# Routing steps of a token group dealt out evenly over the six half-units that may carry them

## The chip, the cores and the metric

The kernel runs on one core of a Trainium2 chip. The metric is the device time of one launch in microseconds (us), the median of the runs shown. Before the change it is 934.42 us (three runs: 934.04, 934.42, 937.76). The profile that is read below is one further execution with its own time, 937.85 us.

The engines are TensorE (PE, with its weight loads as PEld), VectorE (DVE), ScalarE (ACT), GpSimd (POOL) and SyncE (SP), which issues most DMAs. Each engine works through its own list of instructions in order.

## The reference

Linear attention feeds a mixture of experts that sends each token to one expert:

```
proj = x @ w_phi                       # x is q or k: batch 8, heads 8, seq 576, head_dim 64; 128 features
proj -= max|proj| over the features
phi  = [exp(proj), exp(-proj)]         # 256 features
kv = phi(k)^T @ v ; z = sum phi(k)     # per batch and head
out = (phi(q) @ kv) / (phi(q) @ z + 1e-6)

x = out as 4608 tokens x 512
logits = x @ w_gate                    # 8 experts
e = argmax(logits) ; g = softmax(logits)[e]
y = g * (relu(x @ w1[e]) @ w2[e])      # 512 -> 1024 -> 512
```

## The kernel before

**Units and groups.** The attention is cut into 16 units. A unit is two batch rows (a group) and two heads (a pair); four units in a row make a group, and there are four groups. A unit has nine chunks of 128 tokens, taken in pieces 8, 0, 2, 4, 6 (`PIECES`: the last chunk alone, then four pairs of chunks). In what follows "k2" is the piece that begins with chunk 2 of k, "q2" that of q. Every fp32 matmul operand is split in a high part and a remainder (`xh`, `xl`; `kh`, `kl`; `vh`, `vl`; in the experts `wh`, `wl`), and ACT makes the high part, DVE or POOL the remainder.

**One piece.** PE projects (L246 to L248, `ps_proj`, two PSUM buffers), DVE takes the largest magnitude (`mx`, L252) and subtracts it (`t`, L253). For k, ACT makes the exponentials `e` and then `kh` (L273), and POOL or DVE makes `kl` (L275). For q, PE transposes `t` into `pt` (L284) and ACT makes the exponentials `qp` from it. So PE works on a piece, hands it to DVE, and needs DVE's `t` back twice: for the transposes `pt` of a q piece, and before the PSUM buffer of the piece may be used again two pieces later.

**Beside the features** of one unit, PE carries the products of the unit before: `pk` (phi(k)^T v, L315), `pf` (with w_gate folded in, L341) and `pn` (phi(q) times that, L363). Each unit is emitted in two halves, `first_half` and `second_half`, lists of such matmuls that `merge` zips with the feature pieces by their costs. DVE normalises `pn` into `xrow` and the logits' parts `lgc`.

**Routing.** When the first unit of a group has been emitted, the routing of the group before is put on a list of 27 steps, `deferred` (function `route`): logits, the largest, shift, candidates, first of the largest, one-hot, a sum, three empty steps, `count_ranks` (ten small matmuls into `prk` and DVE's `rks`), an empty step, `rank` (`rki`), `rank_parts` (`rkb`, L652, and `rki` again, L653), `rank_values` (POOL casts `blk` and `rkr`, L656 and L657), nine `select` steps (each one DVE instruction `sel_p` and one POOL instruction `sel_h`, L671), and three steps for the gate. For the last full group eleven steps of `lead` follow: they look for the most used expert (`pc`, `lead_e`), mark its first tokens (`bl`, L746), find their rows (54 small matmuls into `pl`) and gather them (`xg`, L774). Three such lists are worked off, in units 5 and 6, in units 9 and 10, and in units 13 to 15. The function `spread` inserts steps between the items of a half: one behind every sixth item, from the seventh on.

**What sets the order.** The lists only say in which order instructions are emitted. A scheduler then places them on each engine by dependences, priorities and its own idea of costs, and it moves an instruction forward when its engine would otherwise be free. What stands where is therefore read from the built program; the section on the change shows such places.

Of the kernel before, what the change touches and what calls it, by code (L numbers as in the profile page):

```python
# [27 lines left out]
NPR = H // 2  # L28
# [19 lines left out]
def tile_linear_attention_moe(  # L48
# [142 lines left out]
    NLAST0, NLAST, AHEAD = 4, 4, 5  # L191
# [69 lines left out]
    def k_features(st, c0, n):  # L261
        t = project(st, "k", c0, n)
        m = 2 * n
        e = work.tile([P, 4, 2, F], F32, name="e", bufs=2)
        A.activation(e[:, 0:m, 0, :], t[:, 0:m, :], AF.Exp)
        A.activation(e[:, 0:m, 1, :], t[:, 0:m, :], AF.Exp, scale=-1.0)
        st["e", c0] = e
# [38 lines left out]
    def kv_steps(st, bb):  # L306


        def step(hh, i, c, j):
            vh, vl = st["v"]  # L310
            if (hh, i, j) == (0, 0, 0):
                st["pk", bb] = ps_kv.tile([P, 2, 2 * F], F32, name="pk", tag="pk")
            n = D if j == 1 else D + 1
            kh, kl, s0 = st["kp", c]
            return T.matmul(  # L315
                st["pk", bb][0:n, hh, :],
                (vl if j == 1 else vh)[:, 2 * (c + (bb if c == 8 else 0)) + hh, 0:n],
                (kl if j == 2 else kh)[:, s0 + hh].rearrange("p s f -> p (s f)"),
                start=(hh, i, j) == (0, 0, 0),
                stop=(hh, i, j) == (1, 4, 2),  # L320
            )

        return [
            (120, lambda a=(hh, i, c, j): step(*a))
            for i, c in enumerate(CHUNKS[bb])
            for hh in range(2)
            for j in range(3)
        ]

    def kv_copy(st, bb):  # L330
        kvT = sm.tile([D + 1, 2, 2 * F], F32, name="kvT")
        A.copy(kvT, st["pk", bb][0 : D + 1])
        st["kvT", bb] = kvT

    def fold_steps(st, bb):


        def step(hh, s):
            if (hh, s) == (0, 0):
                st["pf"] = ps_kv.tile([P, 2, 2, W], F32, name="pf", tag="pk")  # L340
            m = T.matmul(  # L341
                st["pf"][:, hh, s, :],
                st["kvT", bb][:, hh, s * F : (s + 1) * F],
                fold[:, 2 * st["pr"] + hh, :],
                start=True,
                stop=True,
            )
            if (hh, s) == (1, 1):
                st["kf", bb] = sm.tile([P, 2, 2, W], F32, name="kf", bufs=3)
                with tc.high_priority(offset=200):  # L350
                    V.tensor_copy(st["kf", bb], st["pf"])
            return m

        return [(168, lambda a=(hh, s): step(*a)) for hh in range(2) for s in range(2)]

    def num_steps(st, chunks):


        def step(c, hh, bb, s):
            if c % 3 == 0 and hh == 0 and s == 0:  # L360
                st["pn"] = ps_nm.tile([P, 6, W], F32, name="pn")
            qp, s0 = st["qp", c]
            m = T.matmul(  # L363
                st["pn"][:, 2 * (c % 3) + hh, :],
                qp[:, s, s0 + hh, :] if c < 8 else qp[:, s, hh, bb : bb + 2].rearrange("p b q -> p (b q)"),
                st["kf", bb][:, hh, s, :],
                start=(s == 0 and (c < 8 or bb == 0)),
                stop=(s == 1 and (c < 8 or bb == 1)),
            )
            if c % 3 == 2 and hh == 1 and s == 1 and (c < 8 or bb == 1):  # L370
                normalize(st, c - 2, st["pr"])
                if c == 8:
                    eng = G if st["g"] == NG - 1 and st["pr"] == 2 else nc.sync
                    store_rows(st["g"], st["x"], st["pr"] * P, P, eng=eng)
            return m

        return [
            (186, lambda a=(c, hh, bb, s): step(*a))
            for c in chunks
            for hh in range(2)  # L380
            for bb in ([c // 4] if c < 8 else [0, 1])
            for s in range(2)
        ]
# [35 lines left out]
    def ordered(items):  # L419


        def go(f):
            m = f()
            if behind_order[0] is not None:
                tc.add_manual_dep(
                    m.ins,
                    behind_order[0].ins.name,
                    mybir.DependencyInfo(mybir.DependencyClass.NoSync, mybir.DependencyReason.DATA),
                    reason="order of the products",
                )  # L430
            behind_order[0] = m

        return [(t, lambda f=f: go(f)) for t, f in items]

    def half(kv, fo, nu, copy):

        res = kv[:CUT1] + zipped(kv[CUT1:CUT2], fo) + kv[CUT2:CUT3] + zipped(kv[CUT3:], nu)
        return ordered(res) + [(0, copy)]

    def first_half(prev):  # L440
        return half(
            kv_steps(prev, 1), fold_steps(prev, 0), num_steps(prev, range(4)), lambda: kv_copy(prev, 1)
        )

    def second_half(cur, prev):
        if prev is None:
            return ordered(kv_steps(cur, 0)) + [(0, lambda: kv_copy(cur, 0))]
        return half(
            kv_steps(cur, 0), fold_steps(prev, 1), num_steps(prev, range(4, 9)), lambda: kv_copy(cur, 0)
        )  # L450

    def run(steps):
        for f in steps:
            f()

    def spread(items, steps):

        res, k = [], 0
        for i, it in enumerate(items):
            res.append(it)  # L460
            if i >= 6 and i % 6 == 0 and k < len(steps):
                res.append((0, steps[k]))
                k += 1
        del steps[:k]
        return res
# [19 lines left out]
    def feature_items(st, u):  # L485
        ks = {c: (330 * n, lambda c=c, n=n: k_features(st, c, n)) for c, n in PIECES}
        kps = {c: (0, lambda c=c, n=n: k_parts(st, c, n)) for c, n in PIECES}
        qs = {c: (550 * n, lambda c=c, n=n: q_features(st, c, n)) for c, n in PIECES}

        def do(f, *a):  # L490
            return (0, lambda: f(*a))

        if u == 0:
            st["ranges"] = RANGES0
            return first_items(st, ks, kps, qs, do)
        st["ranges"] = [(0, CUT), (CUT, NC * P)]
        items = []
        for part in range(2):
            for x in "kq":
                items += [do(load, st, x, part), do(split, st, x, part, A, G)]  # L500
            if part == 0:
                items += [ks[8], qs[8], kps[8], ks[0], qs[0], kps[0]]
        items.append(do(v_parts, st, u))
        return items + [f for c in (2, 4, 6) for f in (ks[c], qs[c], kps[c])]

    def merge(a, b):
        ta, tb = sum(x[0] for x in a) or 1, sum(x[0] for x in b) or 1
        i = j = 0
        ca = cb = 0.0
        while i < len(a) or j < len(b):  # L510
            if j >= len(b) or (i < len(a) and ca / ta <= cb / tb):
                ca += a[i][0]
                a[i][1]()
                i += 1
            else:
                cb += b[j][0]
                b[j][1]()
                j += 1
# [273 lines left out]
    deferred, prev = [], None  # L792
# [4 lines left out]
    feats = feature_items(units[0], 0)  # L797
    for u, st in enumerate(units):
        steps = deferred if u % NPR else []
        nxt = feature_items(units[u + 1], u + 1) if u + 1 < len(units) else []  # L800
        if u == 0:
            merge(feats[:-NLAST0], [])
            feats = feats[-NLAST0:]
        else:
            merge(feats[:-NLAST], spread(first_half(prev), steps))
            feats = feats[-NLAST:]
        merge(feats + nxt[:AHEAD], spread(second_half(st, prev), steps))
        feats = nxt[AHEAD:]
        prev = st
        if u % NPR == 0 and u > 0:  # L810
            run(deferred)
            deferred = route(st["g"] - 1, units[u - 1]["lgc"], 0, NC)
            if st["g"] == NG - 1:
                deferred += lead()
# [81 lines left out]
    st = {}  # L896
# [322 lines left out]
```

## Time and profile before

| | |
|---|---|
| median of three runs | 934.42 us |
| profiled execution, its own time | 937.85 us |
| its span, first to last instruction | 935.9 us |
| PE busy | 895.8 us (96%) |
| DVE, ACT, POOL busy | 593.1, 591.8, 499.1 us |

The attention units run until about 430 us of the span (the last `pn` matmuls), and the experts after that. A matmul is pipelined, so its end is modelled and neighbours overlap. The DVE and POOL durations are spans: an instruction that its engine has begun but that is kept from going on is shown long. [...]

### The profile page before, as it was taken

The page shows a single profiled execution, that of the slowest core. Times are in us where ns is not written, and L with a number is a line of the kernel's source. Part 1 is how long each engine was busy: PE and PEld are TensorE (multiplying, and loading weights), DVE is VectorE, ACT ScalarE, POOL GpSimd, SP SyncE. Part 2 cuts the span into 40 slices and gives each one's busy share as a digit, 9 for nine tenths or more (in the row PEclk, how much of TensorE's full clock was granted, in tenths as well). Part 3 has the DMA queues.
Part 4 walks back from the last instruction along what each step waited for, and adds up shares of the span by engine and source line. Part 5 has one row for each costly group of instructions (what it writes and reads, how often), then busy time and mean ns, then how long its engine had stood idle before and what let it go on. Part 6 is the DMA issues. An engine that isn't in the chain of part 4 may idle for free. (4 is left out here: it accounts for less than half of the span.)

```text
span 935.9 us, 18394 instructions
## 1 busy us (share of the span) xinstructions
PE 895.8 (96%) x6824; PEld 839.3 (90%) x6824; DVE 593.1 (63%) x1016; ACT 591.8 (63%) x895; POOL 499.1 (53%) x355
## 2 busy tenths in 40 slices
PE   5999998999899999999799999999999999999995
PEld 4899998999899989999699999999999999987884
DVE  6777778777887778859754444444444444457850
ACT  5877775878677766756455555555555555568961
POOL 6666668766686669553433333333333333346641
PEclk9999999999999999999999999999999999999998
DMA  4333333333223333143133143431434634664100
GB/s 125 117 105 100 99 106 94 99 98 94 67 89 104 105 105 92 42 150 116 42 126 117 46 158 114 158 113 46 152 113 158 216 114 149 225 208 133 45 24 15
DMA packets 64349, 102.38 MB, mean 109 GB/s; under 512 B 10687, under 2 KB 28479, under 8 KB 64257
## 3 DMA queue, kind: packets, MB, share of 16 engines
q1 hardware_dynamic: 56928, 80.34, 27.7%
q0 software_dynamic: 6720, 20.80, 7.1%
q8 instruction: 54, 0.88, 0.4%
q14 instruction: 39, 0.31, 0.1%
q10 hardware_dynamic: 608, 0.05, 0.0%
HBM read 136.74 MB, written 20.26 MB: 168 GB/s over the span
## 5 line engine op out<-in xcount | busy, mean ns | idle before, releaser
L928 DVE TENSOR_TENSOR wl<-raw,wh 128x1024 fp32r<-128x1024 f32 x137 | 185.7, 1368 | 139.0 <-ACT wh L927 135.6
L927 ACT CAST wh<-raw 128x1024 fp32r<-128x1024 f32 x184 | 191.5, 1049 | 96.1 <-PE po L992 68.3
L928 POOL TENSOR_TENSOR wl<-raw,wh 128x1024 fp32r<-128x1024 f32 x47 | 116.6, 2486 | 173.5 <-ACT wh L927 166.1
L363 PE MATMUL pn<-kf,qp 128*128 128x73 f32 x1024 | 155.3, 254 | 0.0
L970 PE MATMUL pm<-xh,wh 128*128 128x256 f32 x544 | 153.7, 283 | 0.7 <-ACT xh L952 0.7
L971 PE MATMUL pm<-xl,wh 128*128 128x256 f32 x544 | 154.1, 283 | 0.2 <-DVE xl L953 0.2
L972 PE MATMUL pm<-xh,wl 128*128 128x256 f32 x544 | 153.9, 283 | 0.0
L363 PEld LDWEIGHTS pn<-kf,qp 128*128 128x128 f32 x1024 | 149.3, 191 | 0.2
L252 DVE TENSOR_REDUCE mx<-ps_proj 128x4 f32<-128x512 f32 (+1 forms) x160 | 100.6, 631 | 66.3 <-PE ps_proj L248 65.7
L275 POOL TENSOR_TENSOR kl<-e,kh 128x1024 fp32r<-128x1024 f32 x47 | 112.2, 2388 | 40.6 <-ACT kh L273 38.5
L235 POOL TENSOR_TENSOR xl<-xr,xh 128x512 fp32r<-128x512 f32 (+2 forms) x62 | 88.1, 1420 | 52.7 <-ACT xh L234 52.5
L991 PE MATMUL po<-wl,hh 128*128 128x512 f32 x272 | 107.3, 394 | 3.0 <-DVE wl L928 3.0
L990 PE MATMUL po<-wh,hh 128*128 128x512 f32 x272 | 109.8, 404 | 0.0
L970 PEld LDWEIGHTS pm<-xh,wh 128*128 128x128 f32 x544 | 104.1, 191 | 3.3 <-ACT xh L952 0.9
L971 PEld LDWEIGHTS pm<-xl,wh 128*128 128x128 f32 x544 | 104.1, 191 | 2.8 <-DVE xl L953 0.4
L992 PE MATMUL po<-wh,hl 128*128 128x512 f32 x272 | 106.6, 392 | 0.0
L972 PEld LDWEIGHTS pm<-xh,wl 128*128 128x128 f32 x544 | 104.1, 191 | 0.0
L253 DVE TENSOR_TENSOR t<-ps_proj,mx 128x512 f32<-128x512 f32 (+1 forms) x160 | 101.0, 633 | 3.4
L246 PE MATMUL ps_proj<-w_hi,xh 128*128 128x256 f32 x288 | 92.8, 322 | 7.9 <-DVE xh L234 4.3
L315 PE MATMUL pk<-kh,vl 128*64 128x256 f32 x320 | 98.2, 307 | 2.2 <-POOL vl L303 2.2
L315 PE MATMUL pk<-kh,vh 128*65 128x256 f32 x320 | 98.1, 306 | 1.0 <-DVE vh L302 1.0
L315 PE MATMUL pk<-kl,vh 128*65 128x256 f32 x320 | 97.7, 305 | 1.1 <-POOL kl L275 0.7
(217 smaller groups left out, 2023.0 us busy)
## 6 DMA issues: line engine op xcount, KB each, us to landing
raw<-w SPq DMA_DIRECT2D x184, 512.0 KB
vt<-vv SPq DMA_DIRECT2D x16, 640.0 KB
x_dram<-xrow SPq DMA_DIRECT2D x30, 256.0 KB
xr<-kT SPq DMA_DIRECT2D x15, 320.0 KB
xr<-qT SPq DMA_DIRECT2D x15, 320.0 KB
xr<-kT SPq DMA_DIRECT2D x17, 256.0 KB
xr<-qT SPq DMA_DIRECT2D x17, 256.0 KB
x_dram<-xrow SPq DMA_DIRECT2D x32, 32.0 KB
```

Of the source, the lines that this page charges most:

```text
L253: V.tensor_tensor(t[:, 0 : 2 * n, :], psv, mx[:, 0 : 2 * n].unsqueeze(2).to_broadcast([P, 2 * n, F]), op=ALU.subtract,)
L275: eng.tensor_tensor(kl, e[:, 0:m], kh, op=ALU.subtract)
L315: return T.matmul(st["pk", bb][0:n, hh, :], (vl if j == 1 else vh)[:, 2 * (c + (bb if c == 8 else 0)) + hh, 0:n], (kl if j == 2 else kh)[: ...
L363: m = T.matmul(st["pn"][:, 2 * (c % 3) + hh, :], qp[:, s, s0 + hh, :] if c < 8 else qp[:, s, hh, bb : bb + 2].rearrange("p b q -> p (b q)" ...
L927: A.copy(th, raw[k])
L928: (G if k in (POOL_LO if u else POOL_LO0) else V).tensor_tensor(tl, raw[k], th, op=ALU.subtract)
L970: T.matmul(pm[:, i], th, xh[:, k, :], start=(k == 0), stop=False)
L971: T.matmul(pm[:, i], th, xl[:, k, :], start=False, stop=False)
L972: T.matmul(pm[:, i], tl, xh[:, k, :], start=False, stop=(k == KD - 1))
L990: T.matmul(po, hh[:, i, r], th[:, c], start=(i == j == 0), stop=False)
L991: T.matmul(po, hh[:, i, r], tl[:, c], start=False, stop=False)
L992: T.matmul(po, hl[:, i, r], th[:, c], start=False, stop=(i == 1 and j == 3))
```

## The change

`spread` gets the number of half-units that are left for the list, `halves`, and inserts that share of the steps, rounded up, at even distances in the half, instead of one behind every sixth item. For the first unit after the list is made there are six halves left, then five, and so on down to one.

```diff
-    def spread(items, steps):
-
+    def spread(items, steps, halves):
+
+        n = -(-len(steps) // halves) if halves else 0
         res, k = [], 0
         for i, it in enumerate(items):
             res.append(it)
-            if i >= 6 and i % 6 == 0 and k < len(steps):
+            while k < n and (k + 1) * len(items) <= (i + 1) * (n + 1):
                 res.append((0, steps[k]))
                 k += 1
         del steps[:k]
         return res
...
         steps = deferred if u % NPR else []
+        halves = 2 * (NPR - u % NPR) if u % NPR else 0
...
-            merge(feats[:-NLAST], spread(first_half(prev), steps))
+            merge(feats[:-NLAST], spread(first_half(prev), steps, halves))
             feats = feats[-NLAST:]
-        merge(feats + nxt[:AHEAD], spread(second_half(st, prev), steps))
+        merge(feats + nxt[:AHEAD], spread(second_half(st, prev), steps, max(0, halves - 1)))
```

A first half has 51 items and a second 59. Before, they took eight and nine steps, so the 27 steps were emitted in 8, 9, 8 and 2, and the 38 with `lead` in 8, 9, 8, 9 and 4. Now the 27 go out in 5, 5, 5, 4, 4, 4 and the 38 in 7, 7, 6, 6, 6, 6. The instructions are the same ones. The steps from the logits to the one-hot and the gate keep their places on DVE and POOL: these lists are alike row by row in both programs up to and with `RECIPROCAL se`. What moves stands behind them.

DVE before, where the ranks of the first group are made, in the second half of unit 5 (`t_2086` is k6 and `t_2137` q6 of that unit):

```order
L253 TENSOR_TENSOR t_2086<-ps_proj_2078,mx_2085 128x512
L644 TENSOR_TENSOR rks_2126<-prk_2115,onehot_138 128x72
L648 TENSOR_REDUCE rki_2165<-rks_2126 128x9
L252 TENSOR_REDUCE mx_2136<-ps_proj_2129 128x4
L652 TENSOR_SCALAR rkb_2173<-rki_2165 128x9
L253 TENSOR_TENSOR t_2137<-ps_proj_2129,mx_2136 128x512
L390 TENSOR_SCALAR rec_2157<-pn_2064 128x6
L653 TENSOR_SCALAR rki_2165<-rki_2165 128x9
```

DVE now, where the same steps stand, in the first half of unit 6 (`t_2250` is k0, `t_2285` q0, `t_2334` k2, `t_2356` q2):

```order
L253 TENSOR_TENSOR t_2250<-ps_proj_2242,mx_2249 128x512
L645 TENSOR_TENSOR rks_2270<-prk_2259,onehot_138 128x72
L252 TENSOR_REDUCE mx_2284<-ps_proj_2277 128x4
L649 TENSOR_REDUCE rki_2345<-rks_2270 128x9
L253 TENSOR_TENSOR t_2285<-ps_proj_2277,mx_2284 128x512
L252 TENSOR_REDUCE mx_2333<-ps_proj_2326 128x4
L653 TENSOR_SCALAR rkb_2374<-rki_2345 128x9
L253 TENSOR_TENSOR t_2334<-ps_proj_2326,mx_2333 128x512
L654 TENSOR_SCALAR rki_2345<-rki_2345 128x9
L252 TENSOR_REDUCE mx_2355<-ps_proj_2348 128x4
L672 TENSOR_SCALAR sel_p_142<-iota_pb_130,rkr_2430,part1_133 128x128
L253 TENSOR_TENSOR t_2356<-ps_proj_2348,mx_2355 128x512
```

The rank steps have moved by about half a unit, and the nine `sel_p`, one row of nine before, are now dealt out one by one between the `mx` and `t` of q2, k4, q4, k6 and q6. The second group has the same rows in unit 10.

POOL before, from the remainders at the end of unit 5 on:

```order
L303 TENSOR_TENSOR vl0_158<-vt_2340,vh0_156 128x1280
L617 CAST base_b_3484<-base_144 128x8
L656 CAST blk_141<-rkb_2173 128x9
L235 TENSOR_TENSOR xl_2331<-xr_2328,xh_2330 128x512
L657 CAST rkr_2183<-rki_2165 128x9
L671 TENSOR_SCALAR sel_h_143<-iota_pb_130,rkr_2183,hbase_135 128x128 x4
L275 TENSOR_TENSOR kl_2195<-e_2089,kh_2194 128x1024
L671 TENSOR_SCALAR sel_h_143<-iota_pb_130,rkr_2183,hbase_135 128x128 x5
L235 TENSOR_TENSOR xl_2337<-xr_2334,xh_2336 128x512
L275 TENSOR_TENSOR kl_2325<-e_2278,kh_2324 128x1024
```

POOL now, the same stretch (`kl_2307` is that of k0 of unit 6, made from `t_2250`):

```order
L303 TENSOR_TENSOR vl0_158<-vt_2322,vh0_156 128x1280
L235 TENSOR_TENSOR xl_2313<-xr_2310,xh_2312 128x512
L275 TENSOR_TENSOR kl_2172<-e_2081,kh_2171 128x1024
L618 CAST base_b_3555<-base_144 128x8
L275 TENSOR_TENSOR kl_2307<-e_2253,kh_2306 128x1024
L235 TENSOR_TENSOR xl_2319<-xr_2316,xh_2318 128x512
L657 CAST blk_141<-rkb_2374 128x9
L658 CAST rkr_2430<-rki_2345 128x9
L672 TENSOR_SCALAR sel_h_143<-iota_pb_130,rkr_2430,hbase_135 128x128 x9
L235 TENSOR_TENSOR xl_2554<-xr_2551,xh_2553 128x640
L275 TENSOR_TENSOR kl_2443<-e_2394,kh_2442 128x1024
L235 TENSOR_TENSOR xl_2560<-xr_2557,xh_2559 128x640
```

The cast `rkr`, which the first `sel_p` on DVE waits for, now stands behind `kl` of k0 and one more `xl`. The nine `sel_h` follow each other without a break, and the three remainders behind them come in one go.

In the third list (unit 13) the ranks stay in the second half. There DVE now has `rkb`, `rki` and five `sel_p` in a row ahead of k8 of unit 14, and POOL stands like this:

```order
L235 TENSOR_TENSOR xl_5235<-xr_5232,xh_5234 128x512
L657 CAST blk_141<-rkb_5127 128x9
L275 TENSOR_TENSOR kl_5099<-e_5001,kh_5098 128x1024
L658 CAST rkr_5189<-rki_5091 128x9
L672 TENSOR_SCALAR sel_h_143<-iota_pb_130,rkr_5189,hbase_135 128x128 x9
```

Before, `blk`, an `xl` of 512 and `rkr` followed each other there; now a `kl` of 1024 stands between `blk` and `rkr`. The steps of `lead` have moved from the last pieces of unit 14 and the first of unit 15 to the middle and the end of unit 15: `bl` from ahead of k8 to ahead of k4, and the 54 `pl` matmuls from behind q0's projection to around q6's transposes.

## Rows read from the trace of the kernel before

**Rows 1.** The page, part 1: busy time, share of the span, instructions
```profile
PE 895.8 (96%) x6824; PEld 839.3 (90%) x6824; DVE 593.1 (63%) x1016; ACT 591.8 (63%) x895; POOL 499.1 (53%) x355
```
**Rows 2.** Stretches: length, busy us (instructions) of each engine, PEclk, DMA share, GB/s
```profile
141.50:145.00 3.50, 3.50 (x19) 3.50 (x20) 3.26 (x9) 2.12 (x4) 2.29 (x3) 0.52 0.26 75
...
170.00:180.00 10.00, 10.00 (x96) 9.99 (x96) 8.15 (x18) 9.59 (x16) 7.18 (x4) 1.00 0.20 55
```
**Rows 3.** Who waited for whom: us in total, times, longest us
```profile
PE pt L284 <- DVE t L253: 9.1, 7, 1.5
```
**Rows 4.** PE in order of time: start us, us, instruction [idle before <-releaser]
```profile
154.56 0.66 PE L284 MATMUL pt<-ident,t 128*128 128x128 f32 x4 [1.52 <-DVE t L253]
...
390.70 0.39 PE L246 MATMUL ps_proj<-w_hi,xh 128*128 128x256 f32 x1 [0.46 <-DVE t L253]
```
**Rows 5.** DVE in order of time, the ranks of the first group
```profile
151.59 2.33 DVE L652 TENSOR_SCALAR rkb<-rki 128x9 int32<-128x9 int32 x1
154.50 0.93 DVE L653 TENSOR_SCALAR rki<-rki 128x9 int32<-128x9 int32 x1
...
156.14 2.15 DVE L671 TENSOR_SCALAR sel_p<-iota_pb,rkr,part 128x128 bf16<-128x128 bf16 x9
```
**Rows 6.** POOL in order of time, the same stretch and the unit behind it
```profile
151.19 2.69 POOL L303 TENSOR_TENSOR vl<-vt,vh 128x1280 fp32r<-128x1280 f32 x1
...
154.13 1.27 POOL L235 TENSOR_TENSOR xl<-xr,xh 128x512 fp32r<-128x512 f32 x1
155.49 0.19 POOL L657 CAST rkr<-rki 128x9 f32<-128x9 int32 x1
155.79 3.41 POOL L671 TENSOR_SCALAR sel_h<-iota_pb,rkr,hbase 128x128 bf16<-128x128 bf16 x4
...
165.84 1.29 POOL L235 TENSOR_TENSOR xl<-xr,xh 128x512 fp32r<-128x512 f32 x1
167.09 2.40 POOL L275 TENSOR_TENSOR kl<-e,kh 128x1024 fp32r<-128x1024 f32 x1
169.44 1.58 POOL L235 TENSOR_TENSOR xl<-xr,xh 128x640 fp32r<-128x640 f32 x1
```
**Rows 7.** One tile's instructions: duration ns min/median/max, first and last start us
```profile
L652 DVE TENSOR_SCALAR rkb<-rki x5: 165/1984/2343, 151.6 to 439.8; 128x9 int32<-128x9 int32 x3, 128x6 int32<-128x6 int32 x1, 128x3 int32<-128x3 int32 x1
...
L671 DVE TENSOR_SCALAR sel_p<-iota_pb,rkr,part x31: 299/307/434, 156.1 to 441.3; 128x128 bf16<-128x128 bf16 x31
```
**Rows 8.** DVE in order of time in unit 6: t of k0, q2 and q4
```profile
163.00 0.68 DVE L253 TENSOR_TENSOR t<-ps_proj,mx 128x512 f32<-128x512 f32 x1
...
167.84 0.69 DVE L253 TENSOR_TENSOR t<-ps_proj,mx 128x512 f32<-128x512 f32 x1
...
173.39 0.69 DVE L253 TENSOR_TENSOR t<-ps_proj,mx 128x512 f32<-128x512 f32 x1
```
**Rows 9.** ACT in order of time: the split ahead of kh of k0, unit 6, and kh
```profile
165.03 0.62 ACT L234 CAST xh<-xr 128x512 fp32r<-128x512 f32 x1
165.56 1.04 ACT L273 CAST kh<-e 128x1024 fp32r<-128x1024 f32 x1
```
**Rows 10.** PE in order of time: transposes of q2 and q6, unit 6; k0's projection, unit 14
```profile
168.81 0.60 PE L284 MATMUL pt<-ident,t 128*128 128x128 f32 x4
...
178.90 0.60 PE L284 MATMUL pt<-ident,t 128*128 128x128 f32 x4
...
365.62 0.37 PE L246 MATMUL ps_proj<-w_hi,xh 128*128 128x256 f32 x1
```
**Rows 11.** POOL in order of time, the third list, between blk and rkr
```profile
359.45 1.26 POOL L235 TENSOR_TENSOR xl<-xr,xh 128x512 fp32r<-128x512 f32 x1
```
**Rows 12.** The lead's steps: DVE's bl, and POOL's issue of a gather
```profile
386.86 2.41 DVE L746 TENSOR_SCALAR bl<-choice,ld 128x27 f32<-128x27 f32 x1
...
396.09 1.29 POOL L774 DMA_INDIRECT xg<-x_dram,gidx  x1 [6.85 <-DVE gidx L763]
```
**Rows 13.** PE in order of time: first transposes of a gathered block
```profile
417.93 0.27 PE L950 MATMUL px<-ident,xg 128*128 128x128 f32 x1
```

## The prediction

> **What bounds the kernel now.** I read the busy times first: PE is busy for 895.8 us, 96% of the span, far ahead of DVE with 63% [rows 1]. So an engine other than PE costs time only where PE waits for it. The view of stretches says where that is: in a stretch of a unit without routing PE is busy for 10.00 of 10.00 us with DVE at 8.15 [rows 2]. The list of waits then shows one kind that returns: transposes `pt` that wait for DVE's `t`, 9.1 us in seven waits, the longest 1.5 [rows 3]. In order of time they lie where routing is worked off, two to a group and a short one at the lead.
>
> The last one of each group lies at the ranks, and its cause can be read off DVE's rows beside POOL's. DVE's `rkb`, nine numbers per partition, takes 2.33 us and ends at 153.92, within 0.04 of the end of POOL's `vl` (151.19 and 2.69) [rows 5, 6]. `rki` takes 0.93 and ends with POOL's `xl` (154.13 and 1.27). The same `rkb` takes 165 ns where POOL does no such work [rows 7]. So DVE's small step is held until POOL's subtraction is through, `t` of q6 comes late, and PE waits 1.52 us [rows 4]. It is so in all three groups.
>
> [...]
>
> **The first chain of a group does not move.** Logits to one-hot and the gate keep their rows on DVE and POOL although they are emitted later: the scheduler moves them forward as before. Their waits, one of the seven in each group, and what follows stay. [...]
>
> **What is removed.** The waits at the ranks: 3 x 1.52 = 4.6 us, since `rkb` and `rki` no longer stand ahead of q6's `t`, or, in the third group, not ahead of one that is near. In the lead, `bl` was held for 2.41 us [rows 12] ahead of k8 and made PE wait 0.46 [rows 4]; it now stands where POOL's list is thinner. Together 5.1 us.
>
> **What is added in the first and the second group: a wait for `rkr`.** DVE's first `sel_p` stands ahead of `t` of q2 and waits for `rkr`. On POOL `rkr` stands behind `kl` of k0, `xl` and `blk`, and that `kl` waits for `kh` of the very k0 that DVE has just done. Counted from the end of k0's `t` (163.68 [rows 8]): `kh` ends at 166.60, of which 0.53 goes since ACT now has the split behind it [rows 9], so at +2.4. Then 2.40 for `kl`, 1.29 for `xl`, 0.19 each for `blk` and `rkr` [rows 6] and some 0.3 for handing over: +6.8. `sel_p` 0.30 [rows 7] and `t` 0.69: `t` of q2 ends at +7.8. PE had its transposes of q2 at 168.81, +5.1 [rows 10], and the ten `prk` matmuls now ahead of them give it perhaps 0.3 more. That is a wait of 2.4; k0's `t` may come a little earlier against PE, as the nine `sel_p` (2.15) no longer stand ahead of it. I take 2.0, bounds 1.2 and 2.4. Behind the waiting `sel_p` stand q2's `t` and all later pieces; PE needs them at once.
>
> **Added in the same groups: selects held behind the burst.** Nine `sel_h` in a row last 9 x 0.85 = 7.7 us (3.41 for four [rows 6]), to +14.5. Then POOL has `xl` to +16.1, `kl` to +18.5 and `xl` to +20.1 back to back (1.58, 2.40, 1.58). DVE's `t` of q4 ended at 174.08, +10.4 [rows 8]; with PE's wait of 2.0 and four `sel_p` (0.24 each) now at +13.4. A copy and `mx` of k6 bring +14.5. There follow `sel_p`, `t` of k6, `sel_p`, `mx` of q6, `sel_p`, `t` of q6, each `mx` and `t` about 0.7. If the first slips in ahead of `xl`, the second is held to +16.1 and the third, by `kl`, to +18.5, and q6's `t` ends at about +19.5. PE wants it at 178.90, +15.2, plus 2.0 and 0.3: +17.5. Wait 2.0. If the first is held too, 3.6; if none is, +17.5 and nothing. No row shows a `sel_p` beside an `xl` or `kl`: its longest is 0.43 [rows 7]. The nearest row is `rkb`, the same operation on DVE, held in full, so I take 2.0 and keep 0 and 3.6 as ends. POOL itself can bear the burst: the remainders it delays feed projections of the next unit.
>
> **Added in the third group.** There `rkb` ends with `xl` at about 360.5 (360.71 before [rows 11], less a little for a shorter list). `blk`, `kl`, `rkr` and handing over take 0.19 + 2.40 + 0.19 + 0.3: DVE stands still until about 363.6. Five `sel_p` (1.2), then `mx`, `sel_p` and `t` of k8, half pieces: 366.0. PE began k0's projection, which needs k8's PSUM buffer, at 365.62 [rows 10], and would now at 364.1. Wait 1.9, and about 0.6 more at q8 behind a further `sel_p`. I take 2.5, bounds 1.0 and, if a later `sel_p` is held by a `kl`, 4.8.
>
> **The lead.** Its steps now stand between k4's and q4's `mx` and `t`: 0.3, bounds 0 and 1. The gathers start some 17 us later than at 396.09 [rows 12]. The `pl` matmuls end at about 412, POOL's list is free by 413, and PE wants the first block at 417.93 [rows 13]: hidden by a few us, so nothing.
>
> **The sum.** -5.1 + 2 x (2.0 + 2.0) + 2.5 + 0.3 = +5.7 us. The clock is not in it: a wait of 1.5 alone brought no slow stretch, two near each other did in two groups of three. I take no change, bounds -3.4 (both stretches go) and +5 (one more per group). The profiled execution took 937.85 us, 1.95 outside its span, so by it the sum is 943.5. The median shown is 3.43 lower, 934.42, and runs of one kernel lie between 934.04 and 937.76; on that base the forecast is **940.1 us**.
>
> **Rivals.**
> *The selects slip through.* For: beside `sel_h` they are not held, and they are bf16 while all held steps shown have 32-bit operands. Against: same operation as `rkb`. Then 2 x 2.0 + 2.5 + 0.3 - 5.1 = +1.7: about 936.
> *The new waits find cover and the clock stays up.* The price is decided by k0's `t`: if it comes a microsecond earlier against PE, the wait for `rkr` falls to its bound, 1.2, and with no select held the sum is -5.1 + 2.4 + 1.0 + 0 = -1.7; without the slow stretches -5.1, about 929. For it: DVE has 2.15 us less ahead of k0. Against: `rkr` hangs on k0's own `kh`, so POOL's 4.1 us come in any case. This is the one on the other side; say 930.
> *The gather is late.* If `pl` or POOL's list ends 4 us later than I count, the first block lands behind 417.93, and each us is PE's. Price about 4: 944.
> *Every POOL instruction holds a DVE select, `sel_h` too.* Five `sel_p` stand in the burst, and each would wait up to 0.85 us, about 0.4 on average: 2 us per group, 6 in all, 946. The trace speaks against it, as said. [...]
>
> **How the numbers follow.** Forecast 0.55 (936 to 946 for itself), selects slip through 0.25, cover 0.10, gather late 0.05, every instruction holds 0.05. The range for 8 in 10 is 932 to 946: the low end takes in the second rival and part of the third, the bounds of the single waits (3.4 to 17.8 added, 5.1 removed) would reach from 929 to 952 if all fell one way. A change under 0.5% (4.7 us) can't be told from none. Faster by more than that: most of the cover case and a little of the next, 0.11. Slower by more, above 939.1: two thirds of the forecast and the two small rivals, 0.48. Within: 0.41.
>
> **What would show it.** In the changed profile: `choice`, `oh_b` and the gate at the times of before, with the slow clock behind them; no wait of PE at q6 of units 5 and 9; DVE idle ahead of a first `sel_p` with `rkr` as releaser, some 2 us, and PE waiting at q2 (or at k4's projection) of units 6 and 10; single `sel_p` of 1 to 2.4 us that end with an `xl` or `kl` of POOL; in unit 14 DVE idle for about 3 us ahead of five `sel_p`. I am wrong if all `sel_p` stay at 0.3 us, if `rkr` comes before DVE has done `mx` of q2, or if PE's waits in the attention fall below the 9.1 us of before.

## The result and the profile after

The changed kernel took 948.93 us in the median of four executions (943.99, 945.92, 951.95, 959.24), against 934.29 for the kernel before: slower, 1.0122 times the time, with an interval of 1.0092 to 1.0153. The comparison leaves out executions over 1.5% above the fastest of their kernel as disturbed, here the 959.24 and in the run once more 957.44 and 959.32, though the experiments show below that such times are most likely the kernel's own, so its ratios are on the low side. The profiled execution is the fastest, 943.99 us with a span of 941.9, so 6.0 us of span over before. The forecast was 940.1, and 943.5 for the profiled execution.

PE's busy time is up by 2.5 us on [rows 1], which fits a further stretch at the lower clock (below), and its waits are up. Part 1 of the page, then the two groups of PE's waits for `t` between 120 and 460 us (total, times, longest):

```profile
PE 898.3 (95%) x6824; PEld 840.9 (89%) x6824; DVE 595.5 (63%) x1016; ACT 592.8 (63%) x895; POOL 498.0 (53%) x355
```
```profile
PE pt L284 <- DVE t L253: 11.6, 9, 2.3
PE ps_proj L246 <- DVE t L253: 3.9, 6, 1.4
```

The first line answers to [rows 3] with 9.1; the second kind came to 2.3 in four waits before. Together 15.5 against 11.4. In order of time the waits lie here (start, duration, instruction, idle before and releaser); the first is the old one of the first chain, the next three are unit 6, the last three unit 14:

```profile
140.83 1.08 PE L284 MATMUL pt<-ident,t 128*128 128x128 f32 x4 [1.45 <-DVE t L253]
166.30 0.35 PE L246 MATMUL ps_proj<-w_hi,xh 128*128 128x256 f32 x1 [0.34 <-DVE t L253]
168.40 0.63 PE L284 MATMUL pt<-ident,t 128*128 128x128 f32 x4 [1.15 <-DVE t L253]
181.10 0.66 PE L284 MATMUL pt<-ident,t 128*128 128x128 f32 x4 [2.25 <-DVE t L253]
...
371.84 0.39 PE L246 MATMUL ps_proj<-w_hi,xh 128*128 128x256 f32 x1 [1.42 <-DVE t L253]
373.44 0.44 PE L284 MATMUL pt<-ident,t 128*128 128x128 f32 x2 [0.21 <-DVE t L253]
381.14 0.63 PE L284 MATMUL pt<-ident,t 128*128 128x128 f32 x4 [0.21 <-DVE t L253]
```

Unit 10 repeats unit 6 with 0.36, 1.16 and 2.27. The waits at the ranks (1.52, 1.54 and 1.53) and that of 0.46 [rows 4] are gone, with another of 0.23 at the lead. So 9.4 us came (3.74 and 3.79 in the two groups, 1.84 in the third) and 5.3 went.

Why q2 and q6 are late is read off DVE's and POOL's rows of unit 6, side by side. DVE:

```profile
163.36 2.21 DVE L653 TENSOR_SCALAR rkb<-rki 128x9 int32<-128x9 int32 x1
165.48 0.68 DVE L253 TENSOR_TENSOR t<-ps_proj,mx 128x512 f32<-128x512 f32 x1
166.08 0.72 DVE L654 TENSOR_SCALAR rki<-rki 128x9 int32<-128x9 int32 x1
...
167.31 0.34 DVE L672 TENSOR_SCALAR sel_p<-iota_pb,rkr,part 128x128 bf16<-128x128 bf16 x1
...
175.26 1.36 DVE L672 TENSOR_SCALAR sel_p<-iota_pb,rkr,part 128x128 bf16<-128x128 bf16 x1
176.54 0.68 DVE L253 TENSOR_TENSOR t<-ps_proj,mx 128x512 f32<-128x512 f32 x1
177.14 1.82 DVE L672 TENSOR_SCALAR sel_p<-iota_pb,rkr,part 128x128 bf16<-128x128 bf16 x1
...
179.48 0.97 DVE L672 TENSOR_SCALAR sel_p<-iota_pb,rkr,part 128x128 bf16<-128x128 bf16 x1
```
POOL:
```profile
163.16 2.38 POOL L275 TENSOR_TENSOR kl<-e,kh 128x1024 fp32r<-128x1024 f32 x1 [1.89 <-ACT kh L273]
165.49 1.28 POOL L235 TENSOR_TENSOR xl<-xr,xh 128x512 fp32r<-128x512 f32 x1
...
166.87 0.19 POOL L658 CAST rkr<-rki 128x9 f32<-128x9 int32 x1
167.17 7.87 POOL L672 TENSOR_SCALAR sel_h<-iota_pb,rkr,hbase 128x128 bf16<-128x128 bf16 x9
175.00 1.56 POOL L235 TENSOR_TENSOR xl<-xr,xh 128x640 fp32r<-128x640 f32 x1
176.53 2.38 POOL L275 TENSOR_TENSOR kl<-e,kh 128x1024 fp32r<-128x1024 f32 x1
178.87 1.53 POOL L235 TENSOR_TENSOR xl<-xr,xh 128x640 fp32r<-128x640 f32 x1
180.36 2.68 POOL L303 TENSOR_TENSOR vl<-vt,vh 128x1280 fp32r<-128x1280 f32 x1
```

Add start and duration in each row. `rkb` ends at 165.57, `kl` at 165.54; `rki` at 166.80, the 512 `xl` at 166.77; the three long `sel_p` at 176.62, 178.96 and 180.45, POOL's `xl`, `kl`, `xl` at 176.56, 178.91 and 180.40. Each step of DVE is kept until POOL's subtraction is through. Beside the nine `sel_h` a `sel_p` takes 0.34. Over the whole kernel (duration in ns, least, median, most) the longest `sel_p` went from 434 [rows 7] to 2054 (it stands behind the `t` of q6, where PE no longer waits for it):

```profile
L672 DVE TENSOR_SCALAR sel_p<-iota_pb,rkr,part x31: 266/340/2054, 167.3 to 447.3; 128x128 bf16<-128x128 bf16 x31
```

In unit 14 DVE stands still for `rkr` as forecast:

```profile
369.61 1.29 DVE L672 TENSOR_SCALAR sel_p<-iota_pb,rkr,part 128x128 bf16<-128x128 bf16 x5 [2.56 <-POOL rkr L658]
```

The clock makes up the rest. These are the stretches of the attention with the lower clock (columns as in [rows 2]; PEclk, third from the end, is the granted TensorE clock as a share of the full one, and in 2.50 us inside each of the three it is 0.50):

```profile
140.00:145.00 5.00, 4.17 (x25) 4.20 (x25) 4.56 (x12) 2.60 (x5) 3.23 (x4) 0.66 0.19 52
181.00:186.00 5.00, 4.90 (x33) 4.90 (x34) 2.86 (x6) 1.09 (x2) 5.00 (x3) 0.66 0.63 168
287.00:292.00 5.00, 4.78 (x31) 4.78 (x32) 2.97 (x6) 1.08 (x2) 5.00 (x3) 0.66 0.59 165
```

Each costs 5 x 0.34 = 1.7 us. The new two stand behind the waits at q6; before, there were two, behind the first chains of groups one and three, 3.50 us at 0.52 [rows 2] and 4.00 at 0.57:

```profile
346.00:350.00 4.00, 3.03 (x15) 3.06 (x16) 3.56 (x9) 2.52 (x5) 3.00 (x3) 0.57 0.21 53
```

One more: +1.7. With 4.1 us of waits this is 5.8 us. The spans differ by 6.0, and since this execution was already 0.6 ahead at PE's first wait for routing (137.88 against 138.46), some 0.8 us stay unexplained.

### The profile page after: what moved, and what is told of

Same layout as the page of the kernel before. It is cut to its first block, busy times and chain, and to the rows that moved or that the text cites. A ratio compares the mean times of both kernels' runs of the same rounds, so it can differ in the third digit from the quotient of the medians.

```text
span 941.9 us, 18396 instructions
## 1 busy us (share of the span) xinstructions
PE 898.3 (95%) x6824; PEld 840.9 (89%) x6824; DVE 595.5 (63%) x1016; ACT 592.8 (63%) x895; POOL 498.0 (53%) x355
```

## The experiments

Each ratio is against the kernel before, run beside the experiment; its median there was 936.0 to 936.8.

**The changed kernel once more**, in more executions, since 943.99 to 959.24 is a wide spread.

> The changed kernel again, as the base of the others and to see how far its executions differ. [...] If that is all, its median lies at 940 to 943 beside 934.3. If slow stretches come and go from execution to execution, it lies higher and spreads over more than 3 us, and the trace of this run has another number of slow stretches than three in the attention.

The 940 to 943 add to 934.3 what the two profiles differ in: 4.2 us of PE's waits for `t` (15.5 against 11.4) and 1.7 us of one more stretch of the lower clock (5 us at 0.66). Measured: 941.65, 945.68, 950.68, 953.2, 957.44, 959.32; ratio 1.0103 (1.0070 to 1.0136). With the first four, ten executions: four lie at 941.7 to 945.9, three at 950.7 to 953.2, three at 957.4 to 959.3. The profiled one, 953.2, shows what a step is. DVE, POOL and PE of unit 6:

```profile
176.03 9.09 DVE L672 TENSOR_SCALAR sel_p<-iota_pb,rkr,part 128x128 bf16<-128x128 bf16 x1
```
```profile
175.85 1.56 POOL L235 TENSOR_TENSOR xl<-xr,xh 128x640 fp32r<-128x640 f32 x1
...
183.81 1.26 POOL L235 TENSOR_TENSOR xl<-xr,xh 128x512 fp32r<-128x512 f32 x1
```
```profile
169.16 0.63 PE L284 MATMUL pt<-ident,t 128*128 128x128 f32 x4 [1.18 <-DVE t L253]
...
187.42 1.11 PE L284 MATMUL pt<-ident,t 128*128 128x128 f32 x4 [7.79 <-DVE t L253]
...
253.18 0.35 PE L246 MATMUL ps_proj<-w_hi,xh 128*128 128x256 f32 x1 [0.60 <-DVE t L253]
```
```profile
183.00:194.00 11.00, 6.58 (x36) 6.58 (x37) 5.86 (x13) 3.28 (x5) 4.44 (x3) 0.53 0.43 134
```

One `sel_p` is kept from 176.03 to 185.12, over POOL's whole row of five subtractions, to 185.07, not let in at any of the four boundaries. PE waits 7.79 us, and the clock is low for 11 x 0.47 / 0.5 = 10.3 us where it was 3.4. PE stands still in the first 4 of these, where a low clock costs nothing, so the clock costs 3.1 us in place of 1.7. Together that is 5.5 + 1.4 = 6.9 us, and the rows agree: against the first profile the transposes of q2 are 0.76 later (169.16 against 168.40) and the first wait of the next list is 7.63 later (253.18 against 245.55). The second group is as in the profile above (2.27). The rest of the 9.2 us between the spans is not this hold: 0.76 of it is there ahead of it, at the transposes of q2, and 1.6 come behind the wait at 253.18. So the lowest step has such a hold in neither group (as profiled), the middle one in one (as profiled); that the highest has it in both fits, but no execution of the changed kernel was profiled there. What I had taken as the upper end of a hold is no upper end.

**The casts on DVE.** If the wait for `rkr` on POOL is what makes q2 late, it goes when DVE makes `rkr` itself.

```diff
-            X.tensor_copy(blk[:, js], r["rkb"])
-            X.tensor_copy(tile_of("rkr", [P, NC], bufs=2), r["rki"])
+            V.tensor_copy(blk[:, js], r["rkb"])
+            V.tensor_copy(tile_of("rkr", [P, NC], bufs=2), r["rki"])
```

> The changed kernel with the two casts blk and rkr of each list on DVE in place of POOL, so that no sel_p waits for POOL's list. Theory A (rkb and rki are themselves held by the subtractions of POOL beside them, 2.21 and 0.72 us in unit 6, and that alone makes t of k2 and q2 late): PE's waits ahead of k4's projection and q2's transposes in units 6 and 10 stay, 1.2 to 1.9 us a group; only the third list gains, since DVE's 2.56 us of idle time ahead of the five sel_p in unit 14 goes, with PE's 1.42 behind it: 1 to 2 us faster than the changed kernel in all. Theory B (as predicted: the first sel_p waits for rkr behind POOL's kl and xl): the waits at q2 fall below 0.4 us in both groups and the kernel is 4 us faster or more.

Measured 953.58, ratio 1.0157 (1.0122 to 1.0193). At q2 PE still waits 0.34 and 1.32, so `rkr` isn't the reason there. In the third list the idle time for `rkr` goes, but `rki`, 0.17 long in the changed kernel, is now held for 2.29 us beside a `kl`, and PE waits 1.89 where it was 1.42: a miss. In the profiled execution (958.7) both groups have the long hold, 7.43 and 7.47 us, and PE waits 6.1 twice.

**The new spreading in the third list only**; units below 12 keep one step behind every sixth item, which `spread` does here for a negative `halves`.

```diff
+        if u < 12:
+            halves = -1
```

> The new spreading for the third list alone (the one with the lead's steps); the first two lists are spread as before. Theory A (the loss is the held steps of the first two groups): units 5, 6, 9 and 10 are as in the kernel before; in the third list waits of 1.99 us go (1.53 at q6 of unit 13 and 0.46 at k8) and 1.84 come (1.42, 0.21, 0.21 in unit 14), and the second slow stretch there goes, 1.7 us: 932.5 to 934.5, the same as before or up to 2 us faster. Theory C (the later gather or another cost of the third list counts): 936 or more.

Measured 934.35, ratio 0.9987 (0.9973 to 1.0000). The waits in the third list are there (1.42, 0.23, 0.20), and PE waits 0.86 for one gathered block, as it does in the kernel before (0.86); no loss is left: the 1.84 is paid by the 1.53 and 0.69 that go. The loss lies in the first two lists.

**Without the nine `sel_p` in these two** (their tile holds zeros instead):

```diff
             for eng, dst, by in ((V, sel_p, part1), (G, sel_h, hbase[...])):
+                if g < 2 and eng is V:
+                    continue
```

> The changed kernel without DVE's nine sel_p in each of the first two lists (their tile is filled with zeros early on, so the part of the gather's indices that sel_p brings is missing). POOL's burst of nine sel_h and the three subtractions behind it stay. Theory A (sel_p held by POOL's xl, kl and xl make t of q6 late): PE's wait of 2.25 us at q6 of units 6 and 10 goes, and the slow stretch behind each, 1.7 us each: 8 us faster than the changed kernel, while the waits ahead of k4's projection and q2's transposes stay, 0.9 to 1.5 us a group, since rkb and rki are still held. Theory B (sel_p waiting for rkr makes q2 late): these go too, 3 us more. Theory D (the burst delays POOL's own products, and PE waits for those): the waits at q6 stay at 1.5 us or more, and the gain is under 3 us.

Measured 938.17, ratio 1.0021 (1.0008 to 1.0034), no execution above 941.3. The waits at q6 are gone, and so are the steps in the times. Those at q2 stay, 0.34 + 1.13, with nothing that waits for `rkr`; `rkb` is still 2.2 us long there. So the selects make q6 late, and the ranks make q2 late.

**A measuring program** for the hold by itself: six times a DVE step and a reduction of its output, beside five POOL subtractions of 128x640 in a row (line numbers are its own), with the step in several forms, and again beside ten of POOL's selects.

```
for i in range(5): G.tensor_tensor(last, xr, xh, op=ALU.subtract)
for i in range(6): V.tensor_scalar(z, src, red, part, ...); V.tensor_reduce(red, z, ...)
```

> A program that only measures: it computes nothing of the reference and writes zeros. In each of 20 blocks POOL does a row of work and DVE beside it six instructions of one form, each followed by a small reduce. Rows of POOL: five subtractions of 128x640 without a break (1.56 us each in the kernel), or ten selects of 128x128 (0.85 each), or five subtractions that each wait for a copy of ACT in between. Forms of DVE: reduce, the select in bf16, the same in f32, the shift of 128x9 integers, the compare of 128x72, the select from PSUM, into PSUM, with a stride of 2 in its output, a subtraction with one operand in PSUM; the select beside the unbroken row six more times. Theory A1 (a held instruction waits for the end of the one POOL instruction beside it): no select is longer than 1.6 + 0.3 us. Theory A2 (POOL's next instruction can take its place again, so that a held one waits for a break in POOL's row): some selects last 3 to 8 us beside the unbroken row, and none over 2 us beside the row with breaks. Beside POOL's selects, if the kernel's rows hold in general, none is held over 0.5 us. By the kernel's rows the shift and the compare are held as the select is, the reduce and the forms with PSUM as a source are not; of the select into PSUM and with a stride nothing is known.

DVE's step as in the kernel, the step from PSUM, into PSUM, and beside POOL's selects:

```profile
15.97 1.13 DVE L122 TENSOR_SCALAR z<-src,red,part 128x128 bf16<-128x128 bf16 x1
...
54.68 0.41 DVE L139 TENSOR_SCALAR zp<-psrc,red,part 128x128 bf16<-128x128 f32 x1
...
63.97 0.41 DVE L142 TENSOR_SCALAR pdst<-src,red,part 128x128 f32<-128x128 bf16 x1
...
94.56 0.38 DVE L122 TENSOR_SCALAR z<-src,red,part 128x128 bf16<-128x128 bf16 x1
```
```profile
14.04 7.50 POOL L104 TENSOR_TENSOR last<-xr,xh 128x640 f32<-128x640 f32 x5 [1.81 <-DVE xh L93]
```

With both ends in SBUF, a step was kept until the next boundary of POOL's row: 1.13 in bf16 and in f32 (0.32 and 0.34 behind the row's end), 1.33 for two shifts in int32, and 2.31 and 2.78 for two compares of two inputs. With its source or its target in PSUM it wasn't (0.41 each), reductions weren't (0.28 or 0.29 each), and beside POOL's selects it wasn't (0.38). That disposes of two rivals of the prediction: selects don't slip through for being bf16, and `sel_h` doesn't hold them. But here a step was always let in at the first boundary. The long hold isn't in it.

**The one-hot compare on POOL**, in the kernel before, to take a held step off DVE in the first chain:

```diff
-            V.tensor_tensor(oh_b, iota_em..., choice..., op=ALU.is_equal)
+            for c in range(n):
+                G.tensor_scalar(oh_b[:, c, :], iota_em, choice[:, j0 + c : j0 + c + 1], 1.0, ...)
```

> The kernel before with one more edit: the compare that makes oh_b is taken from DVE (one instruction, held 1.66 us by POOL's kl) to POOL (nine of 128x8). If held DVE steps are what PE waits for (theory A), the wait of 1.45 us at the first chain of each list goes, three times, and the slow stretches behind two of them with 1.7 us each: 927 to 930. If the hold only moves to DVE's next step, as that of rkb did in the change studied here: less than 1.5 us, 933 to 934. If POOL's longer list delays its own products: 935 or more.

Measured 950.02, ratio 1.0148 (1.0127 to 1.0169), a miss. DVE's next step of the chain now waits for POOL with q's `t` behind it:

```profile
141.98 0.28 DVE L636 TENSOR_REDUCE gsum<-onehot 128x8 f32<-128x72 f32 x1 [3.77 <-POOL onehot L621]
```

PE waits 3.9 in each group where it was 1.45.

**Without `sel_p` and without `rkb` and `rki`** in the first two lists, in the changed kernel (one more early return in `rank_parts`):

> The changed kernel without sel_p and without rkb and rki in the first two lists (the ranks are not split there, so the gather's indices of these groups are not the right ones). Against the run without sel_p alone (938.2) only the held shift and mask of DVE are gone. Theory A: the waits of 0.34 and 1.13 us ahead of k4's projection and q2's transposes go in both groups, 2.9 us, and with them the slow stretch behind one of them: 933.5 to 936. If they stay, something else makes t of k2 and q2 late.

Measured 952.48, ratio 1.0165 (1.0146 to 1.0183). The waits at q2 are gone as the theory of the holds says, but the time isn't better: with `rkr` early, POOL does all nine `sel_h` (162.14 for 8.08) ahead of a remainder that PE needs:

```profile
173.80 0.58 PE L248 MATMUL ps_proj<-w_hi,xl 128*128 128x256 f32 x1 [5.93 <-POOL xl L235]
```

So the run settles the cause at q2 and nothing about the total: POOL can bear the burst only where no remainder that is due stands behind it.

**A second measuring program**, with POOL's row of the kernel (640, 1024, 640, 1280, 512 columns) and 144 selects that start at shifted moments, to find what decides who gets in.

> A program that only measures: it computes nothing of the reference and writes zeros. 36 blocks with POOL's row of the kernel (subtractions of 640, 1024, 640, 1280 and 512 columns without a break, in some blocks with two or three selects among them) and four bf16 selects of DVE beside it, between reduces of a length that changes from block to block, so that a select meets POOL's row at many different points. In the first such program 52 of 52 held selects were let in at POOL's next boundary, but its instructions were all of one length and met DVE at the same points. Theory A1 (a held select always ends with the POOL instruction beside it): none is longer than one POOL instruction, 3.0 us with the longest. Theory A2 (whether it gets in at a boundary is open each time, as the 9.1 and 7.4 us in the changed kernel say): some are held over two or more, up to 9 us.

No select lasted longer than 2.26 us. Nine casts that prepare the blocks, all begun 0.06 us behind POOL's subtraction, lasted over two of POOL's subtractions; two more that began there were let in at the first boundary, at 2.89. One of each:

```profile
38.58 4.11 DVE L89 CAST src<-xr 128x128 bf16<-128x128 f32 x1 [0.44 <-POOL sh L96]
...
75.59 2.89 DVE L89 CAST src<-xr 128x128 bf16<-128x128 f32 x1 [0.40 <-POOL sh L96]
```

So a step can miss a boundary outside the kernel too; what makes it miss stays open. In the kernel, steps that began 0.15, 0.23 and 0.26 us behind POOL got in at the first boundary, others at 0.18, 0.31 and 0.36 didn't.

**The ranks in PSUM**, in the kernel before and in the changed one: `rki` is reduced into spare columns of the PSUM tile `prk`, and `rkb` and `rki` read it from there. The order of instructions stays.

```diff
+            both = ps_kv.tile([P, n * (E + 1)], I32, name="prk", tag="pk")
+            prk = both[:, 0 : n * E].bitcast(F32).rearrange("p (c e) -> p c e", e=E)
+            r["rki"] = both[:, n * E :]
```

> The kernel before with one more edit: the reduce of the ranks writes into spare columns of prk's PSUM tile, and rkb and rki read from there; the order on each engine is that of before. By the program that only measures, DVE's small steps with a source in PSUM are not held by POOL. Theory A: rkb takes 0.2 us beside POOL's vl in place of 2.33, PE's waits of 1.52 us at q6 of units 5, 9 and 13 go and nothing takes their place, since the nine sel_p behind are not waited for: 4.6 us, 929.5 to 931. If the wait only moves on to the next step: 932.5 to 934.5.

> The changed kernel with the same edit (ranks read from PSUM), order unchanged. It parts the two limits on t of q2 in units 6 and 10. If the held rkb and rki are its only cause, the waits of 0.34 and 1.15 us go, 3.0 us in all. If the first sel_p has to wait for rkr behind POOL's kl and xl in any case (the reason that the prediction gave), the 0.34 goes and the 1.15 stays, now with DVE idle ahead of sel_p and rkr as its releaser: 0.7 us in all. The selects held at q6 stay, with PE waits of 2.3 or of 6 to 8 us: 941 to 955.

In the kernel before: 935.8, ratio 0.9991 (0.9981 to 1.0000). `rkb` takes 0.16 beside `vl` (2.33 in [rows 5]) and the waits of 1.52 are gone, but the first `sel_p` now waits 2.11 for `rkr`, and PE waits 0.26 and 0.60 behind that. In the changed kernel: 943.1, ratio 1.0070 (1.0056 to 1.0084), all five executions between 942.6 and 944.9, so by their times none has the long hold. The 0.34 is gone; q2 still waits 1.48, and now for the reason that the prediction gave:

```profile
166.03 0.32 DVE L681 TENSOR_SCALAR sel_p<-iota_pb,rkr,part 128x128 bf16<-128x128 bf16 x1 [1.69 <-POOL rkr L667]
```

The wait for `rkr` is the second limit at q2, hidden behind the held ranks.

**Everything from PSUM**: ranks, their parts, the casts (by DVE) and the selects' `iota` read from PSUM, in the changed kernel, and in the kernel before with the one-hot too.

```diff
-                    dst[:, j0 + c, :], iota_pb, r["rkr"]...
+                    dst[:, j0 + c, :], r["iota"] if eng is V and final is None else iota_pb, r["rkr"]...
```

> The changed kernel with the DVE steps of each list freed of POOL: the ranks, their shift and mask lie in spare columns of prk's PSUM tile, DVE casts blk and rkr from there itself (so no sel_p waits for POOL's list), and sel_p reads its row of numbers from PSUM too (0.41 us in place of 0.31, never held in the program that only measures). DVE makes 0.4 us for that row and 0.9 for nine selects more per list. Theory A (held steps and the wait for rkr are the whole loss behind the ranks): the waits at k4, q2 and q6 of units 6 and 10 and that at k8 of unit 14 go, 9.2 us in the profiled execution, with the slow stretches behind them, and the runs lie together: 930 to 934, faster than the kernel before. If something else in the spreading costs time (POOL's burst of nine sel_h, or prk's tile now kept until the last sel_p, so that PE waits for a free one): 936 or more, with waits of PE for POOL's xl or for DVE's sel_p.

> The kernel before with the same edit, and the one-hot's compare reading choice from PSUM as well (a second small reduce writes it there), so that POOL's kl does not hold it. Theory A: beside the waits at the ranks (1.52 us, three times) those behind oh_b go (1.45 us, three times), and the two slow stretches that follow them (1.7 us each): 922 to 928. If choice's own wait for POOL's cand (0.61) is all that is left but the tiles kept longer make PE wait, 930 to 936; if it is slower than 936, the PSUM buffers are the bound.

Both missed: 965.82, ratio 1.0309 (1.0283 to 1.0335), and 952.53, ratio 1.0182 (1.0156 to 1.0208). In the first every `sel_p` takes 0.36 to 0.41, none is held. But DVE comes out at other moments, and another step of it, the remainder of k8, now falls beside POOL's row:

```profile
181.21 5.28 DVE L275 TENSOR_TENSOR kl<-e,kh 128x512 fp32r<-128x512 f32 x1 [1.62 <-ACT kh L273]
```
```profile
187.24 0.55 PE L246 MATMUL ps_proj<-w_hi,xh 128*128 128x256 f32 x1 [6.15 <-DVE t L253]
```

In the second, one wait per group of 2.9 us is new at q6: DVE waits 3.50 for POOL's gate step, which stands behind `kl`, `xl` and `vl`:

```profile
151.75 0.22 DVE L696 RECIPROCAL se<-se 128x9 f32<-128x9 f32 x1 [3.50 <-POOL se L693]
```

No version tried beats the kernel before by more than can be measured.

## Why the prediction was right in its mechanism and wrong in the median

The mechanism was right: what the selects gain by leaving the ranks is less than what they lose beside POOL's row. For the profiled execution the sum was 943.5 against 943.99. Term by term:

- **First chain unmoved, and 5.1 removed:** as forecast (1.45 stays; the three at the ranks and the 0.46 are gone, and 0.23 more: 5.3). One reading behind it was loose: the 165 ns of [rows 7], set against `rkb`'s 2.33, belong to the shorter `rkb` of the last list (128x6 and 128x3). At 128x9 the ranks in PSUM give 0.16, so the conclusion stands.
- **2.0 at q2, for `rkr`:** 1.5 (0.34 + 1.15), and the reason failed. I left out that `rkb` and `rki`, moved to unit 6, would stand beside another subtraction, `kl` of k0, and be held there as they had been beside `vl`. DVE was never idle ahead of the first `sel_p` of unit 6. The run without `sel_p` and the one with ranks in PSUM show both limits, a few tenths apart.
- **2.0 at q6, selects held:** 2.25 and 2.27 in the profiled execution, the right reason, with single `sel_p` that end with an `xl` or `kl`. But the upper end, 3.6, took for granted that a held step is let in when one subtraction ends. One that isn't lasts 9.09, PE waits 7.8, and with the longer stretch of low clock the group takes 6.9 us more than with the short holds, in six of ten executions by their times. This is the step that failed: it puts the median 5 us above the profiled execution and above the range of 932 to 946 (without the 959.24 it is 945.92, at the range's end).
- **2.5 in unit 14:** 1.84, with DVE idle 2.56 where 3 were forecast. **The lead's 0.3:** nothing; the gathers stayed hidden.
- **The clock, 0:** +1.7. The bound of -3.4 counted each stretch at 1.7, and the two of before show that (3.5 x 0.48 and 4.0 x 0.43). A wait of 1.5 alone brought no slow stretch, as said (behind the 1.52 of [rows 4] PEclk is 1.00 from 154 to 158); one of 2.25, with the short ones some us ahead of it, did, in both groups. But the same waits don't always have the same effect: behind the first chains (1.45) two of three groups have a stretch in the profile of before and one of three in that of the changed kernel (groups two and three: 1.00 from 240 to 252 and from 346 to 356), and in the run without `sel_p` the 1.14 at q2 of unit 10 is followed by matmuls of twice the length (`ps_proj`, 0.56 for 0.28), the 1.13 in unit 6 by none.

So the waits came out 1.6 us below the sum (4.1 against 5.7) and the clock 1.7 above: the agreement of the profiled execution is partly two errors that cancel. There is luck in the pair of executions as well: the profiled one of before is the slowest of the first five (937.85), that of after the fastest of its first four. From median to median the change is 14.6 us, against 5.7 forecast: the sum holds for an execution without the long hold, and one number for a kernel with several times was the wrong thing to forecast.

That a step is held to the end of the one subtraction beside it was my reading of `rkb` beside `vl`, 2.33 us long [rows 5]. By it the hold at q6 is an estimated 2.7 at most, the length of `vl` (2.68); the 9.09 measured over five instructions decides against it as an upper end. That `sel_h` holds no `sel_p` was read from nine `sel_p` of 2.15 beside four `sel_h` of 3.41 [rows 5, 6], and stands: 0.34 in the changed kernel, 0.38 in the measuring program.

## What to carry to other kernels

Before a step is moved, read what POOL does beside DVE at the new place, and every step that moves with it: a small step that was held here lasted until POOL's subtraction ended (1.36 beside an `xl` of 1.56), or longer, in a row without gaps up to all five of it (9.09). Where such a step is taken out of the row's reach by another engine or another memory, look at once at what is late next: in five of the runs here the hold became a wait for POOL or moved to a neighbouring step. And where times fall in steps, profile one execution of each before a median is believed or forecast.

## What the runs showed of the hardware that was not expected

- A held DVE step isn't always let in at the end of POOL's instruction: 9.09 us over five, 7.43 over four, 5.28 (a remainder of DVE) over three, 4.11 over two in the measuring program, where two of eleven casts with the same start (0.06 behind) were let in at the first end. What decides stays open.
- The same select is held beside POOL's subtractions of two inputs (1.13 beside 1.5 each) and not beside POOL's own selects (0.38 there, 0.34 in the changed kernel), though these read SBUF as well. Why wasn't tried.
- One operand in PSUM, source or target, was enough to free a step: 0.41 where the same select was held for 1.13 in SBUF, and `rkb` 0.16 instead of 2.33.
